# A state-space and MLP block: the first transfers in another order, and everything behind x held until x has landed

## The chip, the cores and the metric

The kernel is one program on one core of a Trainium2 chip. The metric is the device time of an execution in microseconds (us). Beside the runs there is one profiled execution, from which all rows come. The engines are named as the profile names them: PE (TensorE), PEld (its weight loads), DVE (VectorE), ACT (ScalarE), POOL (GpSimd) and SP (SyncE, which only issues transfers).

## The reference

The block has a gated long convolution and a squared-ReLU MLP, each behind a layer norm with a modulation from `c`. Shapes: 2048 positions (S), 640 channels (D), 1728 hidden columns (F), all float32.

```python
def _A_ref(q, k, v, shift_k, ssm_k, ssm_D):
    k_shift = sum(k_pad[:, t:t + S, :] * shift_k[:, ks - 1 - t] for t in range(ks))   # 4 taps, causal
    kv = k_shift * v
    y_f = rfft(kv padded to 2 S) * rfft(ssm_k padded to 2 S)                          # per channel
    y = irfft(y_f)[:S] + kv * ssm_D
    return q * y

mod = (_silu(c) @ w_mod).reshape(c.shape[0], 6, 1, -1)     # sa, ca, ga, sb, cb, gb
h = _layernorm(x) * (1 + ca) + sa
x = x + ga * _A_ref(h, k, v, shift_k, ssm_k, ssm_D)
h = _layernorm(x) * (1 + cb) + sb
x = x + gb * (relu(h @ w1 + b1) ** 2 @ w2 + b2)
```

## The kernel before

**Blocks.** The channels are cut into 5 blocks of 128. For each block the convolution is done by matrix products: two stages of a forward transform (constants `cw`, then `gb`) of the filter (H, from `ssm_k`) and of k·v (x), a product of the two spectra, and two stages back (constants `gi`, then `ca`). gb and gi are 2 MB each and are loaded in four quarters of 512 KB; group 4·i to 4·i+3 of the 16 groups needs quarter i.

**k·v.** `kv_load` fetches 512 rows of k and of v (256 KB each) for one block. `kv_k` transposes k on PE and copies it, scaled by the first tap, on ACT; `kv_s` adds the other taps on DVE (L261, L266); `kv_v` transposes v on PE; `kv_m` multiplies the two on DVE (L283) and stores 256 KB to the DRAM tensor `kv_d`. Block 0 has four such steps (h = 0 to 3), which follow each other on DVE. The transform wants k·v in another layout (64 positions of 4 channels in a row), so it is read back from `kv_d` by `load_x` in four pieces of 256 KB into the tile `p`, half 0; half 1 of the tile holds the filter, loaded by `load_h0` in four pieces of 256 KB. `skip` adds `ssm_D` to the filter's first position on POOL.

**Spectra.** `unit_a(b, i, q)` is the first stage for a quarter of the block (i = 0 for x, 1 for H): 64 matmuls on PE (`pa`, L383) into two PSUM tiles, then two ACT copies into the tile `a`. `spectrum` is the second stage (L398), 8 matmuls for one group. For block 0 the H spectra are made ahead by `early_h(0, j)`, j = 0 to 7 (`eh` in the trace, two groups, 16 matmuls and one ACT copy each). `front(b, j)` makes the x spectrum of the same two groups (`x`), multiplies it with H on DVE and combines on POOL; `back(b, j)` is the first stage of the inverse (`qp`, L464) and reads quarter j of gi.

**Order.** The program is written out in order, and `keep_order` ties each engine's instructions to the order in which they were written. The prologue up to the first `front` is plain code (from L846); behind it a table (`tab`, filled by `at`) says at which slot, FS(b, j) beside `front(b, j)` and GS(b, s) behind them, each further call stands. Nearly all transfers go through `sp_dma` (L136) on the SP queue, and each waits until the transfer four places ahead of it (OUT = 4) has landed. The last phase, from about 290 us, is the MLP; the change doesn't touch it.

The profile's `KV` is the tile that k and v land in, `kacc` is k·v of block 0, `kt` and `vt` are the transposes, `hs` the finished H spectra.

## Time and profile before

| | us |
|---|---|
| three runs | 691.37, 696.17, 697.38 (median 696.17) |
| the profiled execution | 693.38 |
| its span, first to last instruction | 691.6 |
| PE busy in the span | 657.0 (95%) |
| DVE, ACT, POOL busy | 335.9, 330.1, 311.4 |
| moved by DMA | 74.76 MB |

The profile is of one execution. Its span leaves out what lies before the first and behind the last instruction. Starts are counted from the span's start. Busy times are of an engine alone: PE and PEld overlap. [...]

### The profile page before, as it was taken

How to read it: one execution, taken by the hardware profiler on the slowest of the kernel's cores; microseconds unless marked ns; L12 is line 12 of the kernel's file. 1: busy time of each engine (PE TensorE's matmuls, PEld its weight loads, DVE VectorE, ACT ScalarE, POOL GpSimd, SP SyncE). 2: the span in 40 equal slices, each digit the busy share in tenths (PEclk: the TensorE clock that was granted, in tenths of full speed). 3: DMA queues.
4: the chain of work that ended last, by engine and by line, in shares of the span. 5: the costliest groups of instructions: out<-in, count | busy, mean ns of one | idle time of the engine just before them, and what ended most of it. 6: DMA issues, size and time to landing. Idle time of an engine off the chain costs nothing.

```text
span 691.6 us, 21100 instructions
## 1 busy us (share of the span) xinstructions
PE 657.0 (95%) x9164; PEld 630.8 (91%) x9164; DVE 335.9 (49%) x601; ACT 330.1 (48%) x688; POOL 311.4 (45%) x390
## 2 busy tenths in 40 slices
PE   6699898889999999999999999999999999999996
PEld 4689798778898888889999999999999999999996
DVE  5267584658886697487532322323332332422313
ACT  4436656767976976466324333333233233233221
POOL 1062165359869789443523514415325325225213
PEclk9999999999999999999999999999999999999999
DMA  9897998889671643466020010100200200200101
GB/s 234 244 270 230 233 265 233 236 204 233 191 221 34 173 148 113 127 199 181 1 77 1 26 52 1 41 37 1 77 1 1 77 1 1 77 1 1 39 1 39
DMA packets 110960, 74.76 MB, mean 108 GB/s; under 512 B 48658, under 2 KB 96146, under 8 KB 110868
## 3 DMA queue, kind: packets, MB, share of 16 engines
q1 hardware_dynamic: 108912, 72.87, 37.2%
q8 instruction: 72, 1.18, 0.7%
q10 hardware_dynamic: 1892, 0.54, 0.4%
q14 instruction: 20, 0.16, 0.1%
q0 software_dynamic: 64, 0.01, 0.0%
HBM read 58.98 MB, written 14.42 MB: 106 GB/s over the span
## 4 chain that ended last, share of the span: by engine, by line
PE 81%; DVE 6%; ACT 5%; DMA 4%; issue 2%; POOL 1%; DVEq 0%; POOLq 0%; ACTq 0%; SPq 0%
PE acc L790 27%; PE h L720 26%; PE qp L464 5%; PE pa L383 4%; PE x L398 4%; PE y L541 4%; PE h L398 3%; DMA wm<-in_w_mod_dram 3%; PE t L530 2%; PE h L711 1%; PE xtp L685 1%; DVE KV L261 1%; ACT wx L146 1%; DVE kacc L261 1%; PE vt L276 1%
## 5 line engine op out<-in xcount | busy, mean ns | idle before, releaser
L151 POOL TENSOR_TENSOR mtmp<-mtmp 128x256 f32<-128x256 f32 x112 | 71.4, 638 | 244.4 <-ACT mtmp L752 236.5
L720 PE MATMUL h<-xt,w_S 128*128 128x256 f32 x1290 | 167.5, 281 | 1.1 <-DVE w_S L157 1.1
L720 PEld LDWEIGHTS h<-xt,w_S 128*128 128x128 f32 x1290 | 161.7, 190 | 1.3 <-DVE w_S L157 1.3
L790 PE MATMUL acc<-w_S,hring 128*128 128x320 f32 x960 | 156.6, 311 | 0.2 <-DVE hring L157 0.2
L157 DVE TENSOR_TENSOR hring<-mtmp,hring 128x256 fp32r<-128x256 f32 x112 | 65.4, 584 | 168.3 <-ACT hring L146 168.3
L790 PEld LDWEIGHTS acc<-w_S,hring 128*128 128x128 f32 x960 | 141.7, 188 | 0.8 <-DVE hring L157 0.7
L752 ACT ACTIVATE mtmp<-h,b1t 128x256 f32<-128x256 f32 x104 | 49.4, 475 | 174.0 <-PE h L720 170.8
L146 ACT ACTIVATE hring<-mtmp 128x256 fp32r<-128x256 f32 x112 | 46.5, 416 | 48.8 <-POOL mtmp L151 47.5
L383 PE MATMUL pa<-wx,p 64*64 64x64 f32 x2560 | 49.3, 228 | 10.8 <-issue 6.1
L383 PEld LDWEIGHTS pa<-wx,p 64*64 64x64 f32 x2560 | 43.9, 141 | 16.8 <-issue 11.3
L146 ACT ACTIVATE a<-pa 128x512 f32<-128x512 f32 x80 | 43.5, 608 | 19.7 <-PE pa L383 19.2
L151 DVE TENSOR_TENSOR wx<-x,wx 128x512 f32<-128x512 f32 x64 | 40.8, 683 | 18.9 <-PE x L398 7.7
L541 PE MATMUL y<-wx,wx 128*64 128x64 f32 x1280 | 43.9, 224 | 2.9 <-ACT wx L146 1.6
L541 PEld LDWEIGHTS y<-wx,wx 128*64 128x64 f32 x1280 | 39.9, 138 | 7.4 <-issue 3.4
L398 PE MATMUL x<-a,gb 128*64 128x128 f32 x640 | 41.6, 274 | 3.3 <-DVE wx L151 2.1
L687 DVE TENSOR_SCALAR we<-xtp,cbs 128x256 f32<-128x256 f32 x35 | 19.0, 543 | 46.8 <-PE xtp L685 46.8
L398 PEld LDWEIGHTS x<-a,gb 128*64 128x64 f32 x640 | 35.9, 137 | 4.9 <-PE h L398 3.0
L154 POOL TENSOR_TENSOR wm<-wm,wm 128x640 f32<-128x640 f32 x20 | 32.1, 1606 | 16.9 <-ACT wm L341 16.5
L261 DVE SCALAR_TENSOR_TENSOR KV<-kt,tap,KV 128x511 f32<-128x511 f32 (+2 forms) x48 | 35.9, 748 | 7.6 <-ACT ktail L146 6.0
L146 ACT ACTIVATE q<-qp 128x512 f32<-128x512 f32 (+1 forms) x40 | 21.3, 584 | 35.4 <-PE qp L464 35.4
L398 PE MATMUL h<-a,gb 128*64 128x128 f32 x512 | 34.0, 275 | 1.5 <-ACT wx L146 1.5
L790 PE MATMUL acc<-w_WX,hring 128*128 128x320 f32 x192 | 31.4, 312 | 0.0
(142 smaller groups left out, 1014.2 us busy)
## 6 DMA issues: line engine op xcount, KB each, us to landing
wm<-in_w_mod_dram SPq DMA_DIRECT2D x25, 320.0 KB, 4.1
KV<-in_A_k_dram SPq DMA_DIRECT2D x20, 256.0 KB, 4.6
KV<-in_A_v_dram SPq DMA_DIRECT2D x20, 256.0 KB, 4.4
p<-in_A_ssm_k_dram SPq DMA_DIRECT2D x20, 256.0 KB, 4.7
p<-kv_d SPq DMA_DIRECT2D x20, 256.0 KB, 4.1
xp<-in_A_q_dram SPq DMA_DIRECT2D x20, 256.0 KB, 4.3
q<-in_A_q_dram SPq DMA_DIRECT2D x15, 320.0 KB, 4.5
out_dram<-x SPq DMA_DIRECT2D x14, 320.0 KB, 2.2
```

The source lines that it names most:

```text
L146: act.activation(o, i, AF.Copy)
L151: eng.tensor_mul(o, a, b)
L154: eng.tensor_add(o, a, b)
L157: eng.tensor_sub(o, a, b)
L261: dve.scalar_tensor_tensor(o, tk[:, : 512 - t], tap[:, b, t : t + 1], o, op0=ALU.mult, op1=ALU.add)
L383: pe.matmul(t[e][64 * r : 64 * r + 64, g].rearrange("p m d -> p (m d)"), pt[b][l, i, 8 * q + g, :], cw[l, r], start=True, stop=True,)
L398: pe.matmul(t[64 * a : 64 * a + 64, s + r], gb[:, g, r, a], AX[b][i][:, 2 * g + a], start=True, stop=True,)
L464: pe.matmul(t[a][:, u], gi[l, 4 * j + u, r], w[r][l, u % 2], start=(r == 0), stop=(r == 1),)
L541: pe.matmul(y[64 * h : 64 * h + 64, 4 * (g % 2) + i].rearrange("p c l d -> p (c l d)"), tss[g][:, i, 64 * r : 64 * r + 64], ca[:, r, h], s ...
L720: pe.matmul(hps[n, f][:m], WI[1, f][:, a, b], XT[n][:, x, b], start=(b == 0 and i == 0), stop=(b == NB - 1 and i == 2),)
L752: act.activation(r[:m], h[:m], AF.Relu, bias=b1t[:m, f : f + 1])
L790: pe.matmul(acc[2 * s + i], h[:, a, s * P : (s + 1) * P], w[:, y, i * 320 : (i + 1) * 320], start=(f == 0 and ti == 0), stop=(f == NF - 1 ...
```

## The change

The prologue of block 0 is written out anew.

- The first six transfers on SP are k and v of steps 0, 1 and 2; the pieces of H follow behind, the first of them ahead of step 3's k and v, the other three after. Before, each k and v was followed by a piece of H.
- Two quarters of gb now stand ahead of all four stores of k·v. The third, which stood between the stores, is moved behind the loads of x, beside the fourth.
- The rule of four transfers holds only from x on (`limit`). Before that, as many are in flight as the eight landing semaphores allow. The first transfer behind x, gb's third quarter, also waits until the last piece of x has landed (`hold`).
- On PE the transposes of steps 0 to 2 come ahead of the first unit of H. `unit_a` is split into its matmuls (`unit_p`) and its copies (`unit_c`), so that the second copy of the last H unit and of the last x unit can go to DVE. `skip` is placed later in POOL's order, and PSUM tags of the transposes change.
- The H spectra 4 and 5 are moved from the prologue into the slots of `front(0, 1)` and `front(0, 2)`.

```diff
--- before.py
+++ after.py
@@ -131,14 +131,16 @@
     kv_d = dr.tile([D, S], F32, tag="kv_d", name="kv_d")
     x1_d = dr.tile([S, D], F32, tag="x1_d", name="x1_d")
 
-    queued = []
+    queued, limit, hold = [], [], []
 
 
     def sp_dma(o, i):
         sp.dma_start(o, i)
         queued.append(nc.cur_bb.bb.instructions[-1].name)
-        if len(queued) > OUT:
-            info = mybir.DependencyInfo(mybir.DependencyClass.Sync, mybir.DependencyReason.DATA)
+        info = mybir.DependencyInfo(mybir.DependencyClass.Sync, mybir.DependencyReason.DATA)
+        if hold:
+            tc.add_manual_dep(nc.cur_bb.bb.instructions[-1], hold.pop(), info, reason="place in time")
+        if len(queued) > OUT and limit:
             tc.add_manual_dep(nc.cur_bb.bb.instructions[-1], queued[-1 - OUT], info, reason="place in time")
 
     def copy(eng, o, i):
@@ -219,13 +221,13 @@
             )
 
 
-    def kv_load(i):
+    def kv_load(i, w=(0, 1)):
         b, h = divmod(i, 4)
         rows = slice(h * 512, (h + 1) * 512)
         cols = slice(b * P, (b + 1) * P)
         t = KN[h % (4 if b == 0 else 2)]
-        for w, src in ((0, k), (1, v)):
-            sp_dma(t[:, w], src[rows, cols].rearrange("(t p) d -> p t d", p=P))
+        for w in w:
+            sp_dma(t[:, w], (k, v)[w][rows, cols].rearrange("(t p) d -> p t d", p=P))
 
     kt = {}
 
@@ -372,6 +374,9 @@
 
 
     def unit_a(b, i, q):
+        unit_c(b, i, q, unit_p(b, i, q))
+
+    def unit_p(b, i, q):
         t = [
             ps.tile([P, 8, 32, 2], F32, tag="X", name=f"pa_{b}_{i}_{q}_{e}", bufs=4)
             for e in range(2)
@@ -387,10 +392,13 @@
                         start=True,
                         stop=True,
                     )
+        return t
+
+    def unit_c(b, i, q, t, eng=(act, act)):
         for e in range(2):
             c = 64 * e + 16 * q
             o = AX[b][i][:, :, c : c + 16].rearrange("p m (g d) -> p m g d", d=2)
-            copy(act, o, t[e].rearrange("p g m d -> p m g d"))
+            copy(eng[e], o, t[e].rearrange("p g m d -> p m g d"))
 
     def spectrum(t, b, i, g, s):
         for r in range(2):
@@ -840,29 +848,53 @@
 
     def load_h0(i):
         sp_dma(pt[0][:, 1, 8 * i : 8 * i + 8], hsrc[:, 8 * i : 8 * i + 8, :])
-        skip(0, 8 * i, 8 * i + 8)
-
-    def kv_all(h):
-        kv_k(0, h)
-        kv_s(0, h)
-        kv_v(0, h, "T")
-        kv_m(0, h)
-
-    for i in range(4):
-        kv_load(i)
-        load_h0(i)
+
+    kv_load(0, (0,))
+    kv_load(0, (1,))
+    kv_load(1, (0,))
+    kv_load(1, (1,))
+    kv_load(2, (0,))
+    kv_load(2, (1,))
+    load_h0(0)
+    kv_load(3, (0,))
+    kv_load(3, (1,))
+    load_h0(1)
+    load_h0(2)
+    load_h0(3)
     load_gb(0)
-    kv_all(0)
-    unit_a(0, 1, 0)
     load_gb(1)
-    kv_all(1)
-    unit_a(0, 1, 1)
+    kv_k(0, 0, "X")
+    kv_s(0, 0)
+    kv_v(0, 0, "T")
+    kv_m(0, 0)
+    kv_k(0, 1, "X")
+    kv_s(0, 1)
+    kv_v(0, 1, "T")
+    kv_m(0, 1)
+    skip(0, 0, 8)
+    kv_k(0, 2, "X")
+    pa0 = unit_p(0, 1, 0)
+    unit_c(0, 1, 0, pa0)
+    kv_s(0, 2)
+    kv_v(0, 2, "Y")
+    kv_m(0, 2)
+    skip(0, 8, 16)
+    kv_k(0, 3, "X")
+    pa1 = unit_p(0, 1, 1)
+    unit_c(0, 1, 1, pa1)
+    kv_s(0, 3)
+    kv_v(0, 3, "Y")
+    kv_m(0, 3)
+    load_x(0)
+    hold.append(queued[-1])
+    limit.append(1)
+    skip(0, 16, 24)
+    pa2 = unit_p(0, 1, 2)
+    unit_c(0, 1, 2, pa2)
+    skip(0, 24, 32)
+    pa3 = unit_p(0, 1, 3)
+    unit_c(0, 1, 3, pa3, (act, dve))
     load_gb(2)
-    kv_all(2)
-    unit_a(0, 1, 2)
-    kv_all(3)
-    load_x(0)
-    unit_a(0, 1, 3)
     load_gb(3)
     kv_load(4)
     load_gi(0)
@@ -871,10 +903,14 @@
     load_h(1)
     load_gi(2)
     load_gi(3)
-    for j in range(6):
-        early_h(0, j)
-    for g in range(4):
-        unit_a(0, 0, g)
+    early_h(0, 0)
+    early_h(0, 1)
+    early_h(0, 2)
+    early_h(0, 3)
+    unit_a(0, 0, 0)
+    unit_a(0, 0, 1)
+    unit_a(0, 0, 2)
+    unit_c(0, 0, 3, unit_p(0, 0, 3), (act, dve))
     act.dma_start(ct, c.rearrange("o (b p) -> p (o b)", p=P))
     act.dma_start(ca, ca_d.rearrange("p (r h n) -> p r h n", r=2, h=2))
 
@@ -938,6 +974,8 @@
         row1b[0] = sb.tile([P, D], F32, tag="row1", name="gb2row")
         sp_dma(row1b[0], b2.rearrange("(o d) -> o d", o=1).to_broadcast([P, D]))
 
+    at(FS(0, 1), (early_h, 0, 4))
+    at(FS(0, 2), (early_h, 0, 5))
     at(FS(0, 1), (early_h, 0, 6), (kv_k, 1, 0, "T"), (kv_v, 1, 0))
     at(FS(0, 2), (p_tile, 2))
     at(FS(0, 3), (early_h, 0, 7), (kv_s, 1, 0), (kv_m, 1, 0))
```

The SP queue from the first transfer, before, in order of issue. `KV` is k or v, `p_110` from `ssm_k` a piece of H:

```order
L138 DMA KV<-in_A_k_dram 128x4x128
L138 DMA KV<-in_A_v_dram 128x4x128
L138 DMA p_110<-in_A_ssm_k_dram 128x8x64
L138 DMA KV<-in_A_k_dram 128x4x128
L138 DMA KV<-in_A_v_dram 128x4x128
L138 DMA p_110<-in_A_ssm_k_dram 128x8x64
```

In the changed kernel the same place reads:

```order
L138 DMA KV<-in_A_k_dram 128x4x128
L138 DMA KV<-in_A_v_dram 128x4x128
L138 DMA KV<-in_A_k_dram 128x4x128
L138 DMA KV<-in_A_v_dram 128x4x128
L138 DMA KV<-in_A_k_dram 128x4x128
L138 DMA KV<-in_A_v_dram 128x4x128
L138 DMA p_110<-in_A_ssm_k_dram 128x8x64
L138 DMA KV<-in_A_k_dram 128x4x128
L138 DMA KV<-in_A_v_dram 128x4x128
```

The pieces of H have left the places between the pieces of k and v. Further down the same queue, around the stores of k·v (`kv_d<-kacc`) and the loads of x (`p_110<-kv_d`), before:

```order
L138 DMA gb<-in_gb_dram 128x1024
L138 DMA kv_d<-kacc_71 128x512
L138 DMA gb<-in_gb_dram 128x1024
L138 DMA kv_d<-kacc_71 128x512
L138 DMA gb<-in_gb_dram 128x1024
L138 DMA kv_d<-kacc_71 128x512 x2
L138 DMA p_110<-kv_d 128x8x64 x4
L138 DMA gb<-in_gb_dram 128x1024
L138 DMA KV<-in_A_k_dram 128x4x128
```

and now:

```order
L138 DMA p_110<-in_A_ssm_k_dram 128x8x64 x3
L138 DMA gb<-in_gb_dram 128x1024 x2
L138 DMA kv_d<-kacc_71 128x512 x4
L138 DMA p_110<-kv_d 128x8x64 x4
L138 DMA gb<-in_gb_dram 128x1024 x2
L138 DMA KV<-in_A_k_dram 128x4x128
```

One quarter of gb has moved from in front of the last two stores to behind x. On PE, from the first x spectrum on (`eh_0_6` is the H spectrum 6 of block 0, `kt_1_0` and `vt_1_0` the transposes of block 1's first step), before:

```order
L398 MATMUL x_0_0_578<-a0_0_111,gb_95 64x128 x8
L398 MATMUL x_0_1_593<-a0_0_111,gb_95 64x128 x8
L398 MATMUL eh_0_6_606<-a1_0_112,gb_95 64x128 x8
L239 MATMUL kt_1_0_616<-ident_74,KV_70 128x128 x4
L276 MATMUL vt_1_0_627<-ident_74,KV_70 128x128 x4
L398 MATMUL x_0_2_634<-a0_0_111,gb_95 64x128 x8
L398 MATMUL x_0_3_648<-a0_0_111,gb_95 64x128 x8
```

and now:

```order
L406 MATMUL x_0_0_557<-a0_0_111,gb_95 64x128 x8
L406 MATMUL x_0_1_572<-a0_0_111,gb_95 64x128 x8
L406 MATMUL eh_0_4_586<-a1_0_112,gb_95 64x128 x8
L406 MATMUL eh_0_6_596<-a1_0_112,gb_95 64x128 x8
L241 MATMUL kt_1_0_606<-ident_74,KV_70 128x128 x4
L278 MATMUL vt_1_0_617<-ident_74,KV_70 128x128 x4
L406 MATMUL x_0_2_624<-a0_0_111,gb_95 64x128 x8
L406 MATMUL eh_0_5_637<-a1_0_112,gb_95 64x128 x8
L406 MATMUL x_0_3_648<-a0_0_111,gb_95 64x128 x8
```

The H spectra 4 and 5, which stood before x's first transform, now stand between the x spectra.

## Rows read from the trace of the kernel before

**Rows 1.** The page: PE's busy tenths in 40 slices of the span.

```profile
PE   6699898889999999999999999999999999999996
```

**Rows 2.** Stretches: length, busy us (count) by engine, granted clock, DMA share, GB/s.

```profile
0.00:20.00 20.00, 12.16 (x300) 10.02 (x302) 11.59 (x26) 8.73 (x17) 3.25 (x13) 1.00 1.02 242
20.00:40.00 20.00, 14.65 (x399) 13.61 (x396) 3.63 (x7) 8.54 (x16) 0.92 (x2) 0.91 0.87 237
40.00:60.00 20.00, 20.00 (x416) 18.36 (x418) 13.75 (x24) 9.40 (x20) 13.71 (x27) 1.00 0.85 237
...
140.00:160.00 20.00, 18.16 (x326) 16.40 (x326) 11.76 (x23) 14.27 (x29) 12.36 (x14) 1.00 0.85 214
...
2.00:24.60 22.60, 16.44 (x374) 14.03 (x376) 12.19 (x25) 11.16 (x22) 2.40 (x7) 1.00 1.05 261
...
26.60:56.00 29.40, 25.57 (x613) 23.77 (x615) 14.97 (x24) 11.20 (x22) 14.34 (x27) 0.94 1.00 271
56.00:60.00 4.00, 4.00 (x117) 3.65 (x117) 1.07 (x4) 3.15 (x7) 0.30 (x1) 1.00 0.21 60
60.00:77.00 17.00, 15.55 (x395) 14.03 (x388) 13.01 (x28) 10.69 (x21) 2.29 (x7) 1.00 0.87 266
```

**Rows 3.** Chain that ended last, 21 to 40 us: start, us, what.

```profile
21.47 3.14 DMA kv_d<-kacc
...
24.68 2.90 DMA p<-kv_d
...
27.71 5.22 PE pa L383 x214
32.93 1.58 issue
...
35.36 0.48 ACT a L146
...
35.85 0.60 ACT a L146
...
36.50 1.97 PE x L398 x32
38.47 0.87 PE eh L398 x16
...
40.36 1.90 PE x L398 x32
```

**Rows 4.** DVE in order of time: start, us, instruction, idle before and its end.

```profile
11.88 0.75 DVE L261 SCALAR_TENSOR_TENSOR kacc<-kt,tap,kacc 128x511 f32<-128x511 f32 x1 [2.53 <-ACT ktail L146]
```

**Rows 5.** SP queue in order of time, issues (merged neighbours), 12 to 78 us.

```profile
17.93 0.33 SPq L138 DMA_DIRECT2D gb<-in_gb_dram  x1
18.62 3.17 SPq L138 DMA_DIRECT2D kv_d<-kacc  x2
...
31.88 0.34 SPq L138 DMA_DIRECT2D gi<-in_gi_dram  x1
...
77.20 1.90 SPq L138 DMA_DIRECT2D KV<-in_A_k_dram  x1
```

**Rows 6.** PE in order of time: start, us, instructions, idle before.

```profile
19.33 3.78 PE L398 MATMUL eh<-a,gb 128*64 128x128 f32 x64 [1.17 <-ACT a L146]
23.43 1.97 PE L398 MATMUL eh<-a,gb 128*64 128x128 f32 x32 [0.32 <-DMA gb<-in_gb_dram]
...
51.41 2.06 PE L464 MATMUL qp<-we,gi 64*128 64x128 f32 x32
...
77.87 1.63 PE L383 MATMUL pa<-wx,p 64*64 64x64 f32 x96
```

**Rows 7.** DVE copies out of PSUM (L148): ns min/median/max, first and last start.

```profile
L148 DVE COPY up<-y x4: 681/688/692, 232.7 to 245.0; 128x512 f32<-128x512 f32 x4
```

**Rows 8.** What PE waited for, 0 to 200 us: us, times, longest.

```profile
PE pa L383 <- issue: 6.1, 6, 2.0
```

**Rows 9.** Instructions on the tile gb, 0 to 60 us, last line.

```profile
DMA to landing us min/median/max: 5.0/5.2/6.3
```

## The prediction

> **What bounds the kernel now.** I read the page first: TensorE (PE) is busy for 95% of the span, and its first two slices of 40 are as empty as only the last is again [rows 1]. The table by stretches puts a number on that: PE is idle for 7.8 us of the first 20 and for 5.35 us of the next 20, then for nothing at all from 40 to 60 [rows 2]. So of 34.6 us of idle time in the whole span, 13.2 us lie in the prologue, and what the prologue finishes late, a full PE starts late.
>
> The chain of waits says why [rows 3]. It runs through VectorE (DVE), which forms k·v in four steps, then the last store of it to DRAM (21.47, 3.14 us), then the first load of it back as x (24.68, 2.90 us), then the four units of x's first transform on PE (`pa`, 27.71 to 35.36, with 1.58 us in which PE waits for nothing that the profile shows), then two copies on ScalarE (ACT), and at 36.50 the first x spectrum. Two more views say what sets the store's time. On DVE there is one hole, 2.53 us before the second step [rows 4]. And from 2.0 to 24.6 us the DMA engines are full, at 261 GB/s [rows 2]: a piece of 256 KB takes 1.00 us of that, and 12 pieces of k, v and H, three quarters of gb (two pieces each) and four stores make 22 pieces, 22 of the 22.6 us. The SyncE queue (SP) lets a transfer go when the one four before it has landed, so its rows tell landings: gi went at 31.88, when the fourth piece of x was in [rows 5].
>
> **Step 1, the last store of k·v.** k and v come without H between them, PE takes the second k right after the first v, and the 2.53 us hole goes. Then DVE is done at 21.47 − 2.53 = 18.94, and with the row's 3.14 us the store has landed at 22.1. The transfers allow less: gb's third quarter now goes behind x, 20 pieces are left, and the landing comes two pieces of 1.00 us before the old 24.6, at 22.6. Both conditions have to hold, so I take 22.6, a gain of **2.0 us**; the ends are 24.6 (the queue gives nothing) and 22.1. The queue supports it: the landing of gb's first quarter let the transfer at 17.93 go, and that of the store issued next behind it the one at 18.62 [rows 5]. [...]
>
> **Step 2, x and its transform.** Loads and matmuls are the same and move with the store: the fourth x lands at 31.9 − 2.0 = 29.9. The early spectra 0 to 3 still fit before it: four of them took 3.78 us and need the two quarters of gb that stand ahead of the stores [rows 6]. The last copy is split between ACT and DVE. ACT's two took 0.48 + 0.60 us [rows 3]; a DVE copy of that shape takes 0.69 us [rows 7], so beside ACT's one **0.4 us** is saved. The same split on the last H unit lies in the wait for x and counts nothing. Whether the 1.58 us return cannot be seen from before: such waits at this line were six, 6.1 us, the longest 2.0 [rows 8]. Its ends are 0 and 2.0; I keep 1.58, since instructions and traffic stay alike. So the first x spectrum starts at 36.50 − 2.4 = 34.1 (32.5 if the wait goes). [...] The rows have 6.1 us at this line, so I stay with them.
>
> **Step 3, two H spectra behind the first x.** Spectra 4 and 5 were done at 23.43 while PE waited for x [rows 6], for nothing. Now they stand between x spectra, on a PE that is busy for 20.00 of 20 us [rows 2]. One takes 0.87 us [rows 3], so they cost **1.74 us**. ACT, busy for 9.40 of the same 20 us, has room for their copies.
>
> **Step 4, the held transfers.** gb's third quarter waits on SP until the fourth x has landed; the fourth quarter, k and v of the next block, and gi stand behind it. Issued at 29.9 into an empty queue it takes 2.90 us as the first x did [rows 3] and one more piece, 3.9 us; the upper end is gb's own median, 5.2 [rows 9]. So it lands at 33.8, then at 0.97 us a piece (271 GB/s [rows 2]) the fourth quarter at 35.7, k at 36.7, v at 37.7. PE in its new order: x 0 and 1 from 34.1 to 36.1, H 4 to 36.9, H 6 to 37.8, the transposes of k and v (39.34 to 40.36 before, 1.02 together [rows 3]) to 38.9: each finds its data, v's by some 0.7 us. x 2 then starts at 38.9 instead of 40.36, and behind H 5 PE is ahead by 2.4 − 1.74 = **0.7 us**. With the 1.58 gone PE would wait for the fourth quarter and v, reach x 2 at 38.2, and be ahead by 1.3.
>
> **Step 5, what is left of it.** Between 56 and 60 us only 60 GB/s are moved [rows 2], so the two pieces that were put back, and some 2 us of empty queue while gb starts, are made up there. But the next x load stands in a queue that runs at 266 GB/s since 60 [rows 2]. Its first piece landed by 77.20, when the transfer four places behind it went, and PE took it up at 77.87 [rows 5, 6]: 0.7 us of margin. So a lead of PE above 0.7 us becomes a wait there. Sum: −2.0 − 0.4 + 1.74 = −0.7, with 0 to −1.3 around it. The profiled execution took 693.38 us, 1.8 of them outside the span of 691.6; it becomes 692.7.
>
> **The rivals.**
> A, the full gain: the 1.58 us go, gb arrives in time, and the x load moves up with PE, because its stores come from a k·v chain that PE starts. [...] For it: only part of the queue's time from 60 to 77 is full, a share of 0.87 [rows 2]. Against it: PE had no hole from 40 to 60.
> B, slower: the hold comes back as a wait for gi. The third quarter of gi is the 16th piece behind gb's third, and the inverse transform that reads it started at 51.41 [rows 6], 50.7 with the lead. At 0.97 us a piece it lands at 33.8 + 15.5 = 49.3. At the 214 GB/s of the stretch from 140 to 160 [rows 2] a piece takes 1.22 us, it lands at 53.3, PE waits 2.6 us, and the time is 692.7 + 2.6 = 695.3. It decides against the change below 16 × 262,144 B / 16.9 us = 248 GB/s.
> C, x is not earlier: eight transfers in flight instead of four share the same engines, gb's first halves are ahead of all stores, and the last store lands at 24.6 as before. Then −0.4 + 1.74 = 1.3 us more, 694.7. For it: the queue was already full from 2 to 24.6. Against it: two pieces fewer are in it.
>
> **The numbers.** Chances: the forecast 0.55, A 0.20, B 0.13, C 0.12. The runs shown are 691.37, 696.17 and 697.38; the profiled one lies 2.8 us under their median, and the four average 694.6. I set the runs of the changed kernel by that average: 694.6 − 0.7 = 693.9 us. The range takes A's far end (694.6 − 4.0 = 690.6) and B (694.6 + 1.9 = 696.5), and about 0.7 us on either side because medians of such runs differ by more than the effect: 690.0 to 697.2. One per cent, about what a measurement of this kernel can tell from no change, is 6.9 us; no case reaches it. I leave 0.04 for faster and 0.04 for slower, for causes that are not in the rows, and 0.92 for the same.
>
> **What would show it.** Step 1: no hole before DVE's second k step, the last store landing near 22.6. Step 2: the fourth x at about 29.9, first x spectrum near 34.1. Step 3: H 4 and 5 at 0.87 us each between x spectra. Step 4: no PE wait for gb, k or v between 34 and 39. Step 5: a short PE wait for x at about 77. I am wrong if the first x spectrum is under 32 or over 36, if PE waits for gi near 50, or if the lead at 77 is above 1.5 us.

## The result, and the profile after

The changed kernel takes **698.70 us** (median of 22 runs, 695.6 to 704.8) against 696.09 us for the kernel before on the same chip (22 runs, 691.4 to 699.7). The ratio is **1.0045 [1.0025, 1.0066]**: slower by 0.45%, some 3 us (the two medians lie 2.6 us apart). That is less than the 1% set as the bound for a change, but it lies above the range that was forecast (690.0 to 697.2), and its sign is the other one. The profiled execution took 697.38 us, its span 695.6, against 693.38 and 691.6 before. Runs of one kernel lie some 10 us apart, so one trace is one draw; what that means comes with the experiments.

From the page of the changed kernel: PE's busy tenths in 40 slices, the granted clock, and the queue that brings instructions (packets, MB, share).

```profile
PE   6689799999999898999999999999999999999996
...
PEclk9899999999999999999999999999999999999999
...
q8 instruction: 72, 1.18, 0.7%
```

The first slices are as empty as in [rows 1], and the clock's second slice is down to 8 tenths. The stretches of the changed kernel (columns as in [rows 2]) show where:

```profile
0.00:20.00 20.00, 11.51 (x220) 9.42 (x220) 12.86 (x28) 7.30 (x14) 3.25 (x13) 1.00 1.04 257
20.00:40.00 20.00, 13.98 (x404) 13.27 (x406) 1.38 (x2) 7.33 (x13) 0.00 (x0) 0.78 0.83 224
40.00:60.00 20.00, 20.00 (x359) 18.55 (x357) 14.56 (x24) 7.33 (x15) 14.12 (x27) 0.97 0.81 232
22.00:24.00 2.00, 1.14 (x19) 0.98 (x14) 0.69 (x1) 0.60 (x1) 0.00 (x0) 0.50 0.17 41
26.00:28.00 2.00, 2.00 (x26) 2.00 (x24) 0.00 (x0) 0.60 (x1) 0.00 (x0) 0.58 1.29 211
38.00:40.00 2.00, 1.71 (x16) 1.74 (x18) 0.15 (x1) 0.00 (x0) 0.00 (x0) 0.50 0.85 259
```

PE is busy for 11.51 of the first 20 us (12.16 before) and 13.98 of the next 20 (14.65). Up to 40 us it gets through some 624 matmuls instead of 699 [rows 2], of which the two moved spectra are 32. From 22 to nearly 28 us and again from 38 to 40 its clock is granted at 0.50 of full speed (the stretch from 26 to 28 has 0.58 in the mean). The chain of waits of the changed kernel (start, us, what; [rows 3] are its counterpart) tells the story:

```profile
17.28 3.09 issue
20.37 1.85 PE pa L388 x68
...
23.09 5.93 PE eh L406 x64
29.02 1.10 PE pa L388 x64
...
33.30 3.73 issue
...
38.29 3.43 PE x L406 x32
41.72 1.75 PE eh L406 x32
...
44.49 1.02 PE x L406 x16
```

Two pieces named issue, **3.09 and 3.73 us**, in which PE waits for nothing that the profile shows. The first has no counterpart in the trace before; the second took 1.58 [rows 3]. Behind the first, four early H spectra take 5.93 us, where 64 such matmuls took 3.78 [rows 6]; behind the second, two x spectra take 3.43 where they took 1.97 [rows 3]. These stretches lie at about half of full speed, with a granted clock of 0.61 from 23.09 to 29.02 and 0.56 from 38.29 to 41.72; in the trace before it is 1.00 from 19.33 to 23.11 and from 36.50 to 38.47.

What the change was made for did happen. DVE of the changed kernel (columns as in [rows 4]) goes through without the hole of 2.53 us, and its last product starts at 18.17:

```profile
9.29 0.74 DVE L263 SCALAR_TENSOR_TENSOR kacc<-kt,tap,kacc 128x511 f32<-128x511 f32 x1
...
18.17 0.69 DVE L285 TENSOR_TENSOR kacc<-vt,kacc 128x512 f32<-128x512 f32 x1
```

On SP (columns as in [rows 5]) x's loads go at 22.46, by the landing of the last store; they went at 24.68 [rows 3]. gb's third quarter goes at 28.84, when the fourth piece of x is in.

```profile
22.46 2.65 SPq L138 DMA_DIRECT2D p<-kv_d  x4
28.84 0.83 SPq L138 DMA_DIRECT2D gb<-in_gb_dram  x2
```

PE (as in [rows 6]) starts the third `qp` at 56.42 instead of 51.41, and x's transform of the second block at 85.28 instead of 77.87, there after a wait for its data:

```profile
56.42 2.06 PE L472 MATMUL qp<-we,gi 64*128 64x128 f32 x32
...
85.28 3.39 PE L388 MATMUL pa<-wx,p 64*64 64x64 f32 x128 [1.78 <-DMA p<-kv_d]
```

The counterpart of [rows 8], over the whole span: 9.2 us in five waits, the longest 3.7.

```profile
PE pa L388 <- issue: 9.2, 5, 3.7
```

### The profile page after: what moved, and what is told of

It reads as the page before. It is cut to its first block, busy times and chain, and to the rows that moved or that the text cites. A ratio compares the mean times of both kernels' runs of the same rounds, so it can differ in the third digit from the quotient of the medians.

```text
span 695.6 us, 21096 instructions
## 1 busy us (share of the span) xinstructions
PE 661.2 (95%) x9164; PEld 636.1 (91%) x9164; DVE 337.5 (49%) x603; ACT 329.4 (47%) x686; POOL 311.4 (45%) x390
## 3 DMA queue, kind: packets, MB, share of 16 engines
q8 instruction: 72, 1.18, 0.7%
## 4 chain that ended last, share of the span: by engine, by line
PE 88%; DVE 3%; issue 3%; DMA 3%; ACT 2%; POOL 0%; SPq 0%; DVEq 0%; POOLq 0%; ACTq 0%
PE acc L798 27%; PE h L728 26%; PE pa L388 6%; PE y L549 5%; PE x L406 5%; PE qp L472 5%; PE h L406 4%; PE t L538 2%; PE eh L406 1%; PE h L719 1%; PE vt L278 1%; PE xtp L693 1%; PE kt L241 1%; PE gr L964 1%; DMA p<-in_A_ssm_k_dram 1%
## 5 line engine op out<-in xcount | busy, mean ns | idle before, releaser
L148 ACT ACTIVATE hring<-mtmp 128x256 fp32r<-128x256 f32 x112 | 46.6, 416 | 48.8 <-POOL mtmp L153 47.5
L148 ACT ACTIVATE a<-pa 128x512 f32<-128x512 f32 x78 | 42.3, 607 | 18.7 <-PE pa L388 18.4
L406 PE MATMUL x<-a,gb 128*64 128x128 f32 x640 | 43.0, 280 | 2.4 <-DVE wx L153 1.4
L406 PEld LDWEIGHTS x<-a,gb 128*64 128x64 f32 x640 | 37.5, 141 | 3.4 <-PE h L406 1.9
L263 DVE SCALAR_TENSOR_TENSOR KV<-kt,tap,KV 128x511 f32<-128x511 f32 (+2 forms) x48 | 35.9, 748 | 7.6 <-ACT ktail L148 6.0
L148 ACT ACTIVATE q<-qp 128x512 f32<-128x512 f32 (+1 forms) x40 | 21.2, 583 | 33.2 <-PE qp L472 33.1
L159 POOL TENSOR_TENSOR we<-wx 128x256 f32<-128x256 f32 x20 | 16.1, 807 | 36.0 <-DVE wx L153 35.9
```

Of the source, the lines that this page charges most:

```text
L148: act.activation(o, i, AF.Copy)
L159: eng.tensor_sub(o, a, b)
L263: dve.scalar_tensor_tensor(o, tk[:, : 512 - t], tap[:, b, t : t + 1], o, op0=ALU.mult, op1=ALU.add)
L406: pe.matmul(t[64 * a : 64 * a + 64, s + r], gb[:, g, r, a], AX[b][i][:, 2 * g + a], start=True, stop=True,)
```

## The experiments

Ratios are to the kernel before on the same chip, with their 95% interval. "Four in flight" is the rule that each transfer waits for the one four places ahead of it.

### What the waits are

I had two theories for the waits named issue. **F**: PE waits for its own next instructions. Count them: between the ends of successive waits of the kernel before lie (PE and PEld, columns as in [rows 2])

```profile
34.50:80.10 45.60, 42.41 (x1014) 38.73 (x1013) 32.05 (x61) 24.11 (x47) 18.23 (x39) 1.00 0.88 246
80.10:84.30 4.20, 2.88 (x126) 2.51 (x127) 2.75 (x6) 2.22 (x5) 0.00 (x0) 1.00 0.91 264
84.30:131.38 47.08, 42.78 (x1013) 38.85 (x1013) 30.58 (x58) 27.55 (x52) 24.77 (x40) 1.00 0.89 244
```

1014 + 1013, 126 + 127 and 1013 + 1013, and in the changed kernel

```profile
20.30:37.00 16.70, 11.93 (x380) 11.33 (x381) 0.69 (x1) 6.73 (x12) 0.00 (x0) 0.80 0.81 214
37.00:135.70 98.70, 91.83 (x2153) 84.00 (x2152) 65.41 (x123) 55.22 (x106) 43.23 (x80) 0.97 0.84 237
135.70:186.30 50.60, 48.58 (x1141) 43.90 (x1142) 38.83 (x61) 41.20 (x81) 39.08 (x43) 1.00 0.80 214
```

380 + 381, 2153 + 2152 and 1141 + 1142. All are multiples of 253 to 254: 8, 1, 8 and 3, 17, 9 of them. With the instructions that such rows don't count, the trace's list of PE (18470 before, 18467 in the changed kernel, against 18328 in the rows) gives 256, and in both kernels each wait named issue of over 0.6 us ends at number 193 + 256·k of it or at the one behind (449 and 1217 above; I call this number the count). The instruction queue of the page moves 72 packets, 1.18 MB, 16 KB each, and the page's 9164 matmuls and 9164 weight loads are 72 times 254.6. In the order of time the packets go with the blocks one by one. In all 20 traces of this study there are 108 such waits of over 0.6 us, and each ends 1.1 to 1.7 us (median 1.4; 1.1 to 1.5 for the 11 in the traces of before and of the change) behind the end of the packet for the block that starts there: in the changed kernel's trace the packet for count 449 goes from 18.00 to 18.92, and PE runs on at 20.37.

**R**, the rival, was that the waits belong to a place in the work, a buffer or a transfer. Matmuls put in front move the work against the count, so they tell the two apart.

**e4_pad**: 60 small matmuls ahead of the first transpose.

```diff
+    pad = ps.tile([P, 512], F32, tag="T", name="pad", bufs=2)
+    for i in range(60):
+        pe.matmul(pad[0:64, 0:64], ident[0:64, 0:64], ident[0:64, 0:64], start=True, stop=True)
```

> The changed kernel with 60 small matmuls (120 PE instructions with their weight loads) added in front of the first transpose, while PE waits for k. Theory F: the two waits stay at the same instruction counts, so they come 60 matmuls earlier in the work: in x's transform with about 68 of its 256 matmuls left instead of 8, in the H units 60 matmuls earlier. Theory R: they stay where they are in the work, with 8 matmuls left. Time: F 0 to 2 us under the changed kernel (part of the last wait lies beside the ACT copies), R equal within 1 us.

709.38 us, 1.022 [1.0165, 1.0275]. The 60 took 13 us and delayed the first transpose from 4.35 to 14.34, so the time says little. The places say more (PE in order of time). The 60 are 240 instructions, nearly a block, so that two waits lie only 16 instructions behind the old places: 0.74 us at count 705, and 2.20 at 1473, in the x spectra (the other 0.77 of the row's 2.97 is time up to the end of the copy ahead). The third, 2.34 us at count 1217, has no counterpart at its place in the work: 127 matmuls of x's transform are left there, not 8. F had 68, since it took the 60 for 120 instructions; and it had a wait at 449, where there is none.

```profile
39.59 3.46 PE L388 MATMUL pa<-wx,p 64*64 64x64 f32 x127 [2.34 <-issue]
46.02 3.04 PE L406 MATMUL x<-a,gb 128*64 128x128 f32 x32 [2.97 <-issue]
```

**e7_pad30**: 30 of them.

```diff
-    for i in range(60):
+    for i in range(30):
```

> The change, with 30 small matmuls of the identity ahead of the first transpose, in time in which TensorE waits for k anyway: 120 instructions by the count of the engine's rows (a weight load and a matmul for each of two passes), so every boundary comes 120 instructions earlier in the work. Theory F: waits named issue again only at counts of 193 + 256 k; the place in the work that had 3.09 us at count 449 is now count 569 and has none, the place that had 3.73 us at count 1217 is now 1337 and has none; waits of 0.6 to 3 us at count 705 (the last of the H units) and at 1217 (earlier among the matmuls of x) take their place; time 693 to 700. Rival R (the waits belong to places in the work: buffers, transfers): 2.5 to 4 us stay at the same matmuls, counts 569 and 1337.

697.11 us, 1.0021 [0.9992, 1.0049]. The 30 end at 8.0, which still delays k's transpose by 3.6 us. Neither old place waits for instructions any more (counts 569 and 1337, and in e10 below 497 and 1265); waits are 1.27 us at 1217 and 0.82 at 1473, and between them lies one block:

```profile
33.15:39.65 6.50, 4.75 (x126) 4.40 (x126) 3.18 (x5) 1.79 (x3) 1.66 (x4) 1.00 1.01 314
```

R is out. F's 0.6 to 3 us at count 705 did not come.

### Which part of the change brings them

Here the rival is **H**: the loss comes from the hold and from the two spectra behind x, not from the queue. My first version of F blamed the deep queue that the change allows before x. **e1_limit4** keeps four in flight from the start:

```diff
-    queued, limit, hold = [], [], []
+    queued, limit, hold = [], [1], []
```

> The changed kernel with four transfers in flight from the start instead of eight; order, hold and the moved spectra stay. Theory F (PE's instructions come in blocks of 256; the next block arrives late when many transfers are in flight, and PE stands still with nothing to wait for): the 3.09 us in the H units falls under 1.5 us, the early spectra 0 to 3 end before 27 instead of 28.95, the first x spectrum starts at 36 to 37 instead of 38.29, time 1 to 3 us under the changed kernel's 698.7. Theory H (the loss is the two moved spectra and the hold): the first x spectrum starts no earlier than 38 and the time is that of the changed kernel within 1 us.

693.26 us, 0.9988 [0.9958, 1.0018]. Its chain of waits:

```profile
16.37 2.61 issue
...
32.64 1.46 issue
...
35.37 3.17 PE x L406 x32
```

The wait at 1217 is back to 1.46, the time to that of the kernel before. But the wait at 449 is 2.61, not under 1.5: that one is not from the deep queue.

**e5_before_deep** is the other half of this, the kernel before with the deep queue:

```diff
-    queued = []
+    queued, limit = [], []
...
-        if len(queued) > OUT:
+        if len(queued) > OUT and limit:
...
     load_x(0)
+    limit.append(1)
```

> The kernel before, with its own order of loads, but without the rule of four in flight until x's loads have been issued (from there on four again). Theory F (TensorE waits for its own next block of 256 instructions, whose 16 KB come late when the sixteen engines have a deep queue of data): the queue that in the change stood ahead of the fetch for count 449 is now here too, so TensorE has idle time named issue of 1.5 to 3.5 us at its count of 449 (before it is under 0.4), the early spectra start 1.5 to 3 us later than 19.3 and part of them at a granted clock near 0.5; the time 1 to 4 us over the kernel before on the same chip. Rival H (the loss is due to the hold and the two moved spectra alone): no idle time over 0.6 at count 449, within 1 us of the kernel before.

697.22 us, 1.002 [0.9991, 1.005]. There is no wait at 449. All that PE waits for instructions at this line in the first 60 us is

```profile
PE pa L383 <- issue: 1.2, 1, 1.2
```

so this expectation of F fell. The wait at 449 belongs to the order of the work: all kernels with the new order and nothing in front have it (2.27 to 3.43 us), all four traces with the old order have not. In the old order PE passes count 193 at 11.6 us and reaches 449 at 15; in the new one it passes 193 at 14.39, and reaches 449 already at 17.06, since two units of 64 matmuls come with little between them. In that time only data moves (DMA queues, packets, MB, share; 14.40 to 17.95, then 17.95 to 19.00):

```profile
q1 hardware_dynamic: 498, 1.16, 102.8%
...
q1 hardware_dynamic: 217, 0.40, 99.3%
q8 instruction: 1, 0.02, 5.5%
```

The packet of instructions comes only when PE has run out of them: it goes from 18.00 to 18.92. **e12_gb1_late** asks whether it is the amount of data: the second quarter of gb goes behind the third store.

```diff
     load_gb(0)
-    load_gb(1)
...
     kv_m(0, 2)
+    load_gb(1)
```

> The change with the second quarter of gb (512 KB) issued behind the third store of k.v instead of ahead of the first, so that 0.5 MB less stands in the queues when TensorE passes count 193 at about 14.4. Theory T (traffic delays the fetch): the fetch of the next 16 KB, in the change 3.6 us behind the crossing, begins 1 to 2.2 us behind it, and the wait at 449 falls from 3.1 to 0.5 to 1.8; early spectra 2 and 3 may then wait 0 to 1.5 us for their quarter; 0 to 2 us under the change. Rival P (only the place and the density of the instructions count): lag and wait within 0.6 us of the change's, time the same or up to 1.5 us over it.

696.55 us, 1.0032 [1.0003, 1.0062]; the fetch began 3.4 us behind the crossing, and both waits stayed (PE in order of time):

```profile
19.72 2.19 PE L388 MATMUL pa<-wx,p 64*64 64x64 f32 x68 [3.16 <-issue]
...
37.02 0.49 PE L388 MATMUL pa<-wx,p 64*64 64x64 f32 x8 [3.92 <-issue]
```

So 0.5 MB less in the queues did not shorten them: theory T in this form fell. Its rival P, by which only the place and the density of the instructions count, came out: the wait at 449 is 3.16, in the change 3.09.

Six runs take the hold, the queue and the moved spectra apart. **e2_hold_pa** holds gb's third quarter longer, to the last matmul of x's transform:

```diff
+    pa_x3 = unit_p(0, 0, 3)
+    hold[:] = [nc.cur_bb.bb.instructions[-1].name]
+    unit_c(0, 0, 3, pa_x3, (act, dve))
     load_gb(2)
     load_gb(3)
...
```

> The changed kernel with gb's third quarter, and all behind it, held until the last matmul of x's first transform instead of the landing of x. Theory F: with no other transfer beside x's first transform the 3.73 us in it fall under 1.2 us, x's first spectrum starts at 35 to 36; then PE waits 2 to 4 us for gb before H spectrum 4, and the time is within 2 us of the changed kernel. If the wait belongs to the work itself (theory R: the order of the units, not the traffic), it stays at 3 to 4 us and the time is 3 us or more above the changed kernel.

699.16 us, 1.0055 [1.0018, 1.0092]. With next to no data moving in x's transform (8 GB/s from 30 to 32 us, 0 from 32 to 34; 305 and 356 in the change) the wait at 1217 is 0.67, and what it gives goes into waits for gb and k:

```profile
34.43 0.35 PE L388 MATMUL pa<-wx,p 64*64 64x64 f32 x8 [0.67 <-issue]
...
38.68 1.09 PE L406 MATMUL eh<-a,gb 128*64 128x128 f32 x16 [1.01 <-DMA gb<-in_gb_dram]
40.81 1.09 PE L406 MATMUL eh<-a,gb 128*64 128x128 f32 x16 [1.04 <-DMA gb<-in_gb_dram]
43.13 0.66 PE L241 MATMUL kt<-ident,KV 128*128 128x128 f32 x4 [1.23 <-DMA KV<-in_A_k_dram]
```

**e3_gb2_back** has gb's third quarter behind the last store, holds nothing, and makes spectra 4 and 5 in the prologue; the queue stays deep.

```diff
+    load_gb(2)
     load_x(0)
-    hold.append(queued[-1])
...
-    load_gb(2)
     load_gb(3)
...
+    early_h(0, 4)
+    early_h(0, 5)
...
-    at(FS(0, 1), (early_h, 0, 4))
-    at(FS(0, 2), (early_h, 0, 5))
```

> The changed kernel with gb's third quarter right behind the last store, without the hold, and with H spectra 4 and 5 back in the prologue behind 0 to 3. Theory H: the 1.74 us of the moved spectra leave the x stage, time 1.7 to 3 us under the changed kernel. Theory F: the 3.09 us in the H units stay, six early spectra end at 31 or later, x's transform starts there, and the time is within 1 us of the changed kernel or above it.

692.97 us, 0.9983 [0.9944, 1.0022]: on H's side, and by more than it gave; F's "within 1 us of the change" fell. The wait at 449 stayed (2.68), that at 1217 is 1.12, and the first x spectra start at 35.75, at a granted 1.00 (34 to 38 us).

**e8_no_hold** takes only the hold away.

```diff
-    hold.append(queued[-1])
```

> The change without the hold: the third quarter of gb and what follows it is issued right behind x's loads, eight in flight until there; spectra 4 and 5 stay where the change put them. Theory F: the fetch for count 1217, which in the change began 3.3 us after count 961 in the burst that the hold lets go at 28.8, begins within 2 us as that burst is over earlier; wait at 1217 falls from 3.7 to 0.5 to 2, first spectrum of x 35 to 37, time 1 to 3 us under the change. Rival M (it is the moved spectra that cost, two spectra more in the row behind x): wait at 1217 within 0.7 of 3.7, time within 1 us of the change.

697.18 us, 1.001 [0.9978, 1.0043], wait at 1217 2.00, first x spectrum at 36.05; as F had it (0.5 to 2, and 35 to 37), though its runs scatter by 10.7 us. **e6_e1_e3** is e1 and e3 together:

```diff
-    queued, limit, hold = [], [], []
+    queued, limit, hold = [], [1], []
...
+    load_gb(2)
     load_x(0)
-    hold.append(queued[-1])
...
+    early_h(0, 4)
+    early_h(0, 5)
...
-    at(FS(0, 1), (early_h, 0, 4))
-    at(FS(0, 2), (early_h, 0, 5))
```

> The change with both repairs: four in flight from the start, and the third quarter of gb right behind the last store of k.v, nothing held, spectra 4 and 5 back in the prologue. What is left of the change is the order of the loads of k and v and of the copies. Theory F: the wait at count 449 stays 2 to 3 (limit 4 alone left 2.6), at count 1217 under 1.6, first spectrum of x between 34.5 and 36, 0 to 2 us under each repair alone, so 691 to 694 and 0.1 to 0.5 per cent faster than the kernel before. Rival (the two repairs act on the same wait and don't add up): within 0.5 us of each repair alone.

696.27 us, 1.001 [0.9988, 1.0033], wait at 1217 2.12, where F had under 1.6 and a time below each repair alone: the two repairs don't add up. **e18_limit4_no_hold** is e1 without the hold, so that of the three parts only the spectra stay moved:

```diff
-    queued, limit, hold = [], [], []
+    queued, limit, hold = [], [1], []
...
-    hold.append(queued[-1])
```

> Four in flight from the start and no hold, spectra 4 and 5 behind x as in the change: the third of the ways to undo a part. Theory F: wait at 449 2.3 to 3, at 1217 1 to 2.2 (as in the runs with nothing held), time 0.998 to 1.003 of the kernel before. Rival (hold and queue have no part, and it is the two spectra behind x that cost): 1.004 to 1.007, as the change.

695.42 us, 1.0029 [1.0006, 1.0052], wait at 1217 2.62: the time at F's upper end, the wait over its 2.2, and the time over the kernel before by its interval. The moved spectra may have a share by themselves, but it is not shown: e6, which has them back, lies at 1.001, and the two intervals overlap. Nor is a cost of the hold by itself to be seen: with four in flight the version that keeps it (e1, 0.9988) lies lower, not higher. **e17_limit4_again** repeats e1, with the same edit:

> The change with four in flight from the start, the hold kept, once more: its first 10 runs gave 0.9988 of the kernel before, the best of the versions that keep the hold, from a trace in which the fetch for count 1217 came ahead of the burst. Theory F with the burst as its cause: the same as there, 0.9955 to 1.002, wait at 449 near 2.6 and at 1217 under 2. Rival D (the place of the fetch against the burst is drawn, and the first 10 runs were a good draw): 1.002 to 1.006, with waits over 3 at 1217 in this trace or a longest run over 700.

693.61 us, 0.9998 [0.9974, 1.0022], waits 2.31 and 0.92: with the hold kept, the shallow queue brings the change back to the kernel before in both comparisons.

### What one trace is worth

**e9_again** is the change once more, unchanged.

> The change as it is, once more, beside the three below on one chip. Theory: 0.3 to 0.65 per cent over the kernel before; waits named issue of 2.5 to 3.5 us at count 449 and of 1.5 to 4 at 1217; early spectra 0 to 3 in 5 to 6.5 us at a granted clock near 0.5. Rival (the first comparison was a draw from runs that scatter by 5 us): within 0.2 per cent.

698.33 us, **1.006 [1.003, 1.009]**; waits 3.23 and 3.63, early spectra in 5.76 us. The loss and its two waits repeat (PE's waits at the line, whole span):

```profile
PE pa L388 <- issue: 10.6, 6, 3.6
```

**e10_pad12** puts 12 small matmuls in front; they end as k comes in (its transpose starts at 4.13), so that nothing is late, and every boundary lies 48 instructions earlier in the work.

```diff
...
+    for i in range(12):
...
```

> The change with 12 small matmuls ahead of the first transpose (1.35 to about 4.0 us, before k lands at 4.35, so nothing waits for them): 48 instructions, and every boundary of 256 lies 48 earlier in the work, the one at 449 ahead of the last H unit. Theory F (place of the boundary against the time that its fetch has): wait at count 449 falls from 3.1 to 0.5 to 1.8 us, as count 193 is passed 1.5 to 2 us earlier; none at count 497, the old place; early spectra begin 21 to 22.3 and the clock's low stretch is shorter; 1 to 3 us under the change. Rival T (the wait is as long as the traffic of gb lasts, wherever the boundary lies): TensorE resumes at 20 to 20.8 as in the change, the wait at 449 is 3 to 3.8, and the time is the change's.

The trace is better than F promised: no wait at 449 (F had 0.5 to 1.8), early spectra at 19.90 in 3.71 us at a granted 1.00 (20 to 22 us), 0.73 at 1217, the first x spectrum at 32.61, 5.7 us ahead of the change:

```profile
19.90 3.71 PE L406 MATMUL eh<-a,gb 128*64 128x128 f32 x64 [0.84 <-ACT a L148]
...
30.99 0.69 PE L388 MATMUL pa<-wx,p 64*64 64x64 f32 x32 [0.73 <-issue]
32.61 1.64 PE L406 MATMUL x<-a,gb 128*64 128x128 f32 x26 [0.92 <-DVE a L150]
```

The median is 699.28 us, 1.0061 [1.0035, 1.0087], as bad as the change, where F had 1 to 3 us less. The trace was of the fastest of its runs (693.1). **e15_pad12_a** and **e16_pad12_b** are the same kernel, for two more traces.

> The change with 12 small matmuls in front, once more: the trace at hand is of its fastest run (693.1), six under its median of 699.3. Theory F: the prologue is as there (no wait over 0.6 at count 449, early spectra from 19.9 at full clock, 3.7 us), and what makes the other runs longer lies behind the first x: waits of 1.5 to 4 us at 961, 1217, 3265 or 3521 or later boundaries, which the shift of 48 has moved too, and the time lost with a clock near 0.5 behind them. Rival: the wait at 449 is back in the longer runs, at 2.5 to 3.5 us.

> The same kernel again, for a third trace. Theory F: as for the run ahead of it; the sum of the waits named issue is larger by 3 to 7 us in a run near 699 than the 7.0 of the fastest one. Rival: the sum differs by under 2 us, and the time went into other waits (buffers, transfers).

700.89 and 702.90 us. To the early spectra they are like the first; then they wait 3.33 and 3.76 us (e15) and 3.05 and 3.36 (e16) at counts 961 and 1217, and the x spectra behind take 3.68 us in e16, at a granted 0.50 (38 to 44 us), instead of 1.97. All of PE's waits for instructions together are 11.4 and 12.0 us, against 7.1 in the first, as F had it. PE of e16:

```profile
30.74 3.19 PE L388 MATMUL pa<-wx,p 64*64 64x64 f32 x127 [3.05 <-issue]
37.29 1.13 PE L388 MATMUL pa<-wx,p 64*64 64x64 f32 x32 [3.36 <-issue]
39.34 3.68 PE L406 MATMUL x<-a,gb 128*64 128x128 f32 x32 [0.92 <-DVE a L150]
```

The first x spectrum is 6.7 us later than in e10, the end of the span 9.8. Behind what the packet came shows in the DMA queues of e16. PE passed count 705 at 22.17, just before x's loads were issued (22.48); from 22.20 to 28.10 only data goes, from 23.5 on (first line), and the instructions come behind it (second line, 28.10 to 29.40):

```profile
q1 hardware_dynamic: 4077, 1.03, 92.0%
...
q8 instruction: 1, 0.02, 5.8%
```

In e10 PE passed 705 at 21.71, and the packet went at 22.74, as x's data began to move. In e15 it was 22.86 and 29.23. Half a microsecond in one crossing goes with 9.8 in the span. What puts the packet ahead of the loads or behind them is not shown: in all three traces PE passed 705 just before the first load was issued (0.19 us in e10, 0.38 in e15, 0.31 in e16).

**e11_e3_pad12** was the version that all this pointed to, e3 with the 12 matmuls.

```diff
...
+    for i in range(12):
...
+    load_gb(2)
     load_x(0)
-    hold.append(queued[-1])
...
+    early_h(0, 4)
+    early_h(0, 5)
...
-    at(FS(0, 1), (early_h, 0, 4))
-    at(FS(0, 2), (early_h, 0, 5))
```

> The third quarter of gb right behind the last store, nothing held, spectra 4 and 5 in the prologue (as in the run e3), and the 12 small matmuls in front: the version that the runs point to. Theory F: both waits shorter than in the change (449: 0.5 to 1.8, 1217: under 1.5), early spectra from 21 to 22, first spectrum of x 34 to 35.5, time 0.2 to 0.6 per cent under the kernel before. Rival: as e3 alone, within 0.2 per cent of the kernel before, since what the prologue gains is given back at later boundaries.

694.90 us, 1.0015 [0.9988, 1.0042]: no wait at 449, but 1.84 at 961 and 1.97 at 1217 (of which the last 0.80 came behind the ACT copy that PE needed there too). The rival was right; no version here beats the kernel before. **e13_before_a** and **e14_before_b** are the kernel before, for two more traces.

> The kernel before, unchanged, for a second trace of it: its runs lie from 691 to 702 and the one trace at hand is of a run of 693.4, in the lower part. Theory F (the waits for the next 256 instructions are drawn anew in every run, the prologue's from a narrower range in the kernel before): at count 449 no wait over 0.6; at 1217 1 to 3.5; the waits named issue 6 to 9 us in all, growing with the run's time. Rival S (every run waits alike, the scatter has another source): each wait within 0.4 of the first trace, and a longer run is longer in another row.

> The kernel before a third time, for the same question. Theory F: waits at the same counts (449 plus multiples of 256, and at no other), in sizes that differ from the other two traces by up to 2 us each; the first spectrum of x at 35.5 to 38.5. Rival S: sizes within 0.4 of the first trace.

693.83 and 695.30 us. No wait at 449 in either; at 1217 0.41 and 0.91, under F's 1 to 3.5; the sizes differ from the first trace by more than the 0.4 of rival S. PE's waits for instructions at this line are 6.1 [rows 8], 2.9 and, in e14,

```profile
PE pa L383 <- issue: 5.0, 6, 1.9
```

so they differ from run to run. They did not grow with the time, as F had it: the spans are 691.6, 692.0 and 693.5. At 1217 all three stay under 1.6. PE waits 2.3 us for the first piece of x in all three traces (and 0.87 for the second in e14), and in the first of them the packet for count 961 goes from 24.49 to 25.73, PE waits for x from 25.39 to 27.71, and it comes to 961 at 29.82. That the wait for data gives the instructions their time is argued from this, not shown.

All traces side by side (waits for instructions in us by count, "-" for under 0.35; start of the first x spectrum):

| kernel | ratio [95%] | at 449 | at 961 | at 1217 | first x | span |
|---|---|---|---|---|---|---|
| before, e13, e14 | 1 | - | - | 1.58, 0.41, 0.91 | 36.5, 37.9, 35.9 | 691.6, 692.0, 693.5 |
| after, e9 | 1.0045 [1.0025, 1.0066], 1.006 [1.003, 1.009] | 3.09, 3.23 | - | 3.73, 3.63 | 38.3, 38.1 | 695.6, 695.8 |
| e1, e17 (four in flight) | 0.9988 [0.9958, 1.0018], 0.9998 [0.9974, 1.0022] | 2.61, 2.31 | 0.65, - | 1.46, 0.92 | 35.4, 35.3 | 691.0, 692.5 |
| e2 (held longer) | 1.0055 [1.0018, 1.0092] | 3.20 | - | 0.67 | 35.7 | 697.0 |
| e3 (gb, spectra back) | 0.9983 [0.9944, 1.0022] | 2.68 | - | 1.12 | 35.7 | 689.6 |
| e5 (before, deep) | 1.002 [0.9991, 1.005] | - | - | 1.22 | 35.8 | 690.9 |
| e6 (e1 and e3) | 1.001 [0.9988, 1.0033] | 2.46 | - | 2.12 | 37.8 | 693.4 |
| e8 (no hold) | 1.001 [0.9978, 1.0043] | 3.43 | - | 2.00 | 36.0 | 690.7 |
| e10, e15, e16 (12 in front) | 1.0061 [1.0035, 1.0087] | - | -, 3.33, 3.05 | 0.73, 3.76, 3.36 | 32.6, 40.7, 39.3 | 691.3, 699.1, 701.1 |
| e11 (e3, 12 in front) | 1.0015 [0.9988, 1.0042] | - | 1.84 | 1.97 | 35.0 | 694.4 |
| e12 (gb's second later) | 1.0032 [1.0003, 1.0062] | 3.16 | 0.89 | 3.92 | 38.4 | 697.1 |
| e18 (four, no hold) | 1.0029 [1.0006, 1.0052] | 2.27 | - | 2.62 | 36.7 | 694.0 |

Over these 18 traces and that of e7 the start of the first `qp`, behind the first x spectra, and the span go together with a correlation of 0.89 and a slope of 1.01: what a run loses in its first 45 us it has lost at the end. That `qp` starts at 42.2, 43.6 and 43.1 in the kernel before, and at 47.2 and 46.9 in the change, so its loss is larger than what one trace of a kernel differs from the next. The sum of all of PE's waits for instructions is a poorer measure: with the span it has a correlation of 0.43.

## Why the prediction was wrong, point by point

**Step 1 held.** The hole on DVE went, and x's loads were let go at 22.46; 22.6 was forecast, with gains of 0 to 2.5 as bounds.

**Step 2 failed**, and with it the forecast. It said that the early spectra 0 to 3 still fit before x, and kept the 1.58 us at x's transform "since instructions and traffic stay alike". x landed at 28.8, a microsecond earlier than forecast. But PE was not there: 3.09 us without instructions ahead of the last H unit, which the forecast did not have at all, then early spectra at a granted 0.61 (5.93 us instead of 3.78), so that x's transform began at 29.02, where 27.71 − 2.0 = 25.7 was implied. The wait kept at 1.58, with ends of 0 and 2.0, measured 3.73, since PE now takes x's units without waiting for pieces of x and goes through two blocks of instructions in 4.7 us (count 705 at 28.4, 1217 reached at 33.1), where it took 10.2 in the trace before. So the first x spectrum came at 38.29; 34.1 was forecast, and "over 36" was named as the sign of being wrong. What the wait was could be read from the trace before, whose counts between waits are multiples of 253; the sum of such waits [rows 8] did not show it, and I took it for a constant.

Waits for five of the 72 packets of the changed kernel's trace took 9.2 us at this line alone. I used the row for the size of one wait, and did not ask where the next would fall.

**Step 3 was right in size**: 1.74 us, in the chain as 1.75 instead of 0.87 at 41.72 and 0.87 behind 44.49. Two x spectra at a granted 0.56, 3.43 instead of 1.97 us, were not in the sum. They do not belong to the change alone: one of the three traces of the kernel before has them too (3.50 in e14).

**Step 4**: PE waited for none of gb's third, its fourth, k or v, as forecast; but PE was 4 us later than they were planned for, so this was no test of the margins. x 2 started at 44.49; 38.9 was forecast.

**Step 5**: there is a wait for x's data at the second block, 1.78 us at 85.28, of the kind that was named, for a PE that is late and not early. The sum in rows of the two chains, to the first `qp`: x's transform 1.31 later, its wait 2.15 longer, 1.67 of the rest of it shorter (the split copy 0.4 of them), x spectra 1.46 longer, moved spectra 1.74: 4.99, and the `qp` of 51.41 stands at 56.42. Part of the 1.67 is clock: x's transform starts at a granted 0.50 in the trace before (columns as in [rows 2]), and runs at 1.00 in the changed one (28 to 34 us).

```profile
28.00:30.00 2.00, 2.00 (x89) 2.00 (x83) 0.00 (x0) 0.50 (x2) 0.00 (x0) 0.50 1.29 244
```

By the end of the span the loss is 4.0, and 3.1 and 4.2 us in the two comparisons of runs.

**The rivals.** None was it. A (gain) is out by the time, C (x not earlier) by step 1. No run shows the 4.0 us that the range takes as A's far end (2.0 + 0.4 and the 1.58 gone): the wait put at 1.58 measured 3.73, and the lowest ratio of any version is 0.9983 [0.9944, 1.0022] (e3). B has the sign, but PE waited for gi nowhere.

**What stays open.** What the waits are and where they lie is shown. That they set the scatter of runs is shown for the kernel with 12 in front alone (9.8 us between its traces, with the waits at 961 and 1217); for the kernel before it is not. How much of the mean 0.45% each part carries is not. Of the versions with the new order, the hold and the deep queue (e4, late by its 60 matmuls, aside), the change, e2 and e10 lie at 1.0045 to 1.0061, e12 and e7 at 1.0032 and 1.0021; all without one of the two lie at 0.9983 to 1.0029. That the burst that the hold releases at 28.84, just as PE starts x's transform, stands ahead of the fetch, is the reading that fits the traces of the change; in e1 it is released at 30.28, 2.8 us behind the start of the transform, and the packet went at 31.4 instead of 34.5. This is argued, not shown.

## What to carry to other kernels

Before a stage is packed more tightly, count the instructions between waits that the profile can't name: if they come in equal blocks, as the 253 to 254 by the rows did here, ask whether the engine waits for its own program, and whether a wait for data that is taken away (2.32 us for x in the trace before) was only its cover. Then ask what else moves when each block is fetched, and whether a large transfer is released at that moment. And where runs of one kernel lie 10 us apart, take more than one trace before you trust where the time went: the trace with the earliest first x spectrum was of a kernel that is as slow as the change in the median.

## What the runs showed of the hardware that was not expected

- TensorE's instructions came in packets of 16 KB (72 packets, 1.18 MB, on the page of both kernels), one for 256 of the trace's list. A packet took 0.88 to 1.95 us (median 1.05) in the traces of before and of the change. Against the point at which the block before it is entered it started between 2.5 us ahead and 6.4 us behind (median 0.5 behind, over the 1441 packets of all traces; 2.5 ahead to 3.9 behind in these two), latest in e15, behind loads of x that were issued 0.38 us after that point. Where PE waited for it for over 0.6 us, PE went on 1.1 to 1.7 us behind the packet's end. With 64 x 64 matmuls and their weight loads PE went through a block in 2.4 us (count 961 to 1217 in the changed kernel, 30.7 to 33.1).
- Behind a wait of 3.09 us the next four spectra took 5.93 us, 2.15 more than the 3.78 of the trace before: their granted clock was 0.61 in the mean, and 1.00 before. In e10, where no wait for instructions came ahead of them, they took 3.71, at 1.00 (20 to 22 us).
- 64 x 64 fp32 matmuls of the identity came every 109 ns (120 in 13.06 us in e4, two for each of the 60 of the program), while those of x's transform came every 18 ns (248 in 4.34 us in the changed kernel). Why is not shown.
